# 448-row contractions as 64-row matmuls, four accumulators at a time, in a fused attention and MLP kernel

## The chip, the cores and the metric

One core of one Trainium2 chip. Times are device microseconds of one execution. Runs come in a fast and a slower state. The engines are TensorE (PE; its weight loads are PEld), VectorE (DVE), ScalarE (ACT), GpSimd (POOL) and SyncE (SP).

A ratio below is the mean time of one kernel's fast runs over that of the other's fast runs of the same rounds. It is not quite the ratio of the medians, which are quoted beside it.

## The reference

Cut to what matters; 2048 tokens, width 448, MLP width 1792, 16 heads of 28.

```python
xn = layernorm(x)
q, k, v = split(xn @ wqkv)                    # 448-row contractions
pq, pk = phi(q), phi(k)                       # phi(t) = t+1 if t>0 else exp(t)
kv, z = pk^T v, sum(pk)                       # over all tokens, per head
s = (pq kv / pq z) @ wo
h = relu(xn @ w1 + b1) ** 2                   # 448-row contraction
g = silu(h @ w2 + b2)
out = x + s * g
```

## The kernel before

The kernel records operations, and a small list scheduler gives each accumulator (`Buf`) one of eight banks of PSUM, the memory that matmuls write. A bank is free again when the last reader of its accumulator is done; such a reading out is called an evacuation below. One operation of PE is a run of matmuls. Its waits, those for banks included, come before its first matmul, and its semaphore is raised once, after its last:

```python
new = [b for b in op.writes if isinstance(b, Buf) and b.bank is None]
...
    banks = [b for _, b in times[: len(new)]]      # all of them free before the start
    r = max(r, times[len(new) - 1][0])
...
for op in self.order[e]:
    for s, v in waits[op]:
        h.wait_ge(s, v)
    op.emit(h, e).then_inc(op.sem, 16 if op.nbytes else 1)
```

448 rows are three times 128 and once 64. Two accumulators are made together, so that their 64-row leftovers lie in opposite halves of the array and run at the same time. Pairs alternate between halves last and halves first, so that the halves of two pairs meet:

```python
def pe_two(a, b, n, mm, reads, first):
    ...
    def f(e, _):                                   # halves last
        for w in (0, 1):
            for c in range(3):
                mm(e, w, full, c, c == 0, False)   # 128 rows
        mm(e, 0, lo, 3, False, True)               # 64 rows, lower half, bank a
        return mm(e, 1, hi, 3, False, True)        # 64 rows, upper half, bank b
    add("pe", f, reads, [a, b], 7 * MM(n) + 0.05)
```

The tokens go through in four groups of 512: k and v per 128 tokens, q, then fourteen blocks of h. In the middle of each group the kv product of that group (`kvt(g)`) is added to an accumulator that stays in its bank from group 0 until its mask is applied in group 3. So seven banks are left for the rest. ACT empties h (relu) and v (copy). For q and k the bank is read twice, by an exp on ACT and, after a minimum on DVE, by a multiply-maximum on DVE. After the groups come the denominators (`den`), the w2 products (`gg`), the division (`spread`) and the output products (`ss`).

Of the kernel before, what the change touches and what calls it, by code (L numbers as in the profile page):

```python
# [6 lines left out]
ALU = mybir.AluOpType  # L7
AF = mybir.ActivationFunctionType

P = 128  # L10
S, D, F = 2048, 448, 1792
NT, NG, NF = S // 128, S // 512, F // 128
NH, DH = 16, 28
HC = 4
PD = 112
KA = PD + HC

SPLIT64 = True
# [21 lines left out]
class Program:  # L40
# [8 lines left out]
    def add(self, eng, emit, reads=(), writes=(), dur=0.2, alts=(), nbytes=0):  # L49
        op = Op(eng, emit, reads, writes, dur, alts, nbytes)  # L50
        for t in op.reads:
            w = self.writer.get(t)
            if w is not None:
                op.raw.add(w)
            self.readers.setdefault(t, []).append(op)
        for t in op.writes:
            w = self.writer.get(t)
            if w is not None and w is not op:
                op.deps.add(w)
            for r in self.readers.get(t, ()):  # L60
                if r is not op:
                    op.deps.add(r)
            self.writer[t] = op
            self.readers[t] = [r for r in self.readers.get(t, ()) if r is op]
        op.raw.discard(op)
        op.deps |= op.raw
        for d in op.deps:
            d.succ.append(op)
        self.ops.append(op)
        return op  # L70
# [194 lines left out]
def bass_recurrent_scan__linear_attn_block__dense_activation_squared_relu__prompt_kernel(  # L265
    nc, A_x, A_wqkv, A_wo, B_x, B_w1, B_b1, B_w2, B_b2, out
):
    with ExitStack() as es:
# [3 lines left out]
        add = pr.add  # L272
# [9 lines left out]
        xT = sb("xT", [P, 4, S], bf)  # L282
        w_qkv = sb("w_qkv", [P, 4, 3 * D], bf)
        w_1 = sb("w_1", [P, 4, F], bf)
# [3 lines left out]
        b1f = sb("b1f", [P, NF], f32)  # L288
# [6 lines left out]
        pqT = sb("pqT", [P, 4, S], bf)  # L295
        pk = sb("pk", [P, NT, D], bf)
        va = sb("va", [P, NT, 4, KA], bf)
        r2 = sb("r2", [P, NF, S], bf)
# [5 lines left out]
        obuf = sb("obuf", [P, 8, D], bf)  # L304
        pbank = [es.enter_context(nc.psum_tensor(f"pb{i}", [P, 512], f32)) for i in range(PSUM_BANKS)]

        ps = lambda b: pbank[b.bank]


# [184 lines left out]

        MM = lambda n: n / 2400 + 0.003

        def pe_two(a, b, n, mm, reads, first):

            if not SPLIT64:
                for w, buf in ((0, a), (1, b)):  # L500

                    def f(e, _, w=w):
                        for c in range(4):
                            last = mm(e, w, slice(0, PD), c, c == 0, c == 3)
                        return last

                    add("pe", f, reads, [buf], 4 * MM(n))
                return
            lo, hi, full = slice(0, 64), slice(64, 128), slice(0, 128)
            if first:  # L510

                def f(e, _):
                    mm(e, 0, lo, 3, True, False)
                    mm(e, 1, hi, 3, True, False)
                    for c in range(3):
                        last = mm(e, 0, full, c, False, c == 2)
                    return last

                def f2(e, _):
                    for c in range(3):  # L520
                        last = mm(e, 1, full, c, False, c == 2)
                    return last

                add("pe", f, reads, [a, b], 4 * MM(n) + 0.05)
                add("pe", f2, reads, [b], 3 * MM(n))
            else:

                def f(e, _):
                    for w in (0, 1):
                        for c in range(3):  # L530
                            mm(e, w, full, c, c == 0, False)
                    mm(e, 0, lo, 3, False, True)
                    return mm(e, 1, hi, 3, False, True)

                add("pe", f, reads, [a, b], 7 * MM(n) + 0.05)

        flip = [False]

        def nextflip():
            flip[0] = not flip[0]  # L540
            return not flip[0]

        def phi(buf, slot, tile, rows, n):

# [18 lines left out]
            )  # L563

        def kv(si):
            kb, vb = Buf("K"), Buf("V")

            def mm(e, w, rows, c, start, stop):
                col = D * (1 + w)
                return e.matmul(  # L570
                    ps((kb, vb)[w])[:, 0:D], xT[rows, c, si * P : (si + 1) * P], w_qkv[rows, c, col : col + D],
                    start=start, stop=stop,
                )

            pe_two(kb, vb, D, mm, [("xT", si)] + wnames("wqkv"), nextflip())
            phi(kb, pk[:, si, :], ("pk", si), P, D)
            add(
                "act",
                lambda e, _: e.activation(
                    out=va[:, si, :, 0:PD], in_=ps(vb)[:, 0:D].rearrange("p (c j) -> p c j", c=4), func=AF.Copy  # L580
                ),
                [vb], [("va", si)], 0.547,
            )

        def qq(g, m):
            bufs = (Buf("Q"), Buf("Q"))

            def mm(e, w, rows, c, start, stop):
                col = (m + w) * PD
                return e.matmul(  # L590
                    ps(bufs[w])[0:PD, 0:512], w_qkv[rows, c, col : col + PD], xT[rows, c, g * 512 : (g + 1) * 512],
                    start=start, stop=stop,
                )

            pe_two(*bufs, 512, mm, [("xT", 4 * g + i) for i in range(4)] + wnames("wqkv"), nextflip())
            for w in (0, 1):
                phi(bufs[w], pqT[0:PD, m + w, g * 512 : (g + 1) * 512], ("pq", g, m + w), PD, 512)

        def hh(g, f0):
            bufs = (Buf("H"), Buf("H"))  # L600

            def mm(e, w, rows, c, start, stop):
                col = (f0 + w) * P
                return e.matmul(  # L604
                    ps(bufs[w])[:, 0:512], w_1[rows, c, col : col + P], xT[rows, c, g * 512 : (g + 1) * 512],
                    start=start, stop=stop,
                )

            pe_two(*bufs, 512, mm, [("xT", 4 * g + i) for i in range(4)] + wnames("w1"), nextflip())
            for w in (0, 1):  # L610
                fi = f0 + w
                slot = r2[:, fi, g * 512 : (g + 1) * 512]
                add(
                    "act",
                    lambda e, _, fi=fi, slot=slot, buf=bufs[w]: e.activation(  # L615
                        out=slot, in_=ps(buf)[:, 0:512], func=AF.Relu, bias=b1f[:, fi : fi + 1]
                    ),
                    [bufs[w], "b1f"], [("r2", g, fi)], 0.688,
                )

                def sq(e, eng, slot=slot):
                    if eng == "dve":
                        return e.tensor_tensor(out=slot, in0=slot, in1=slot, op=ALU.mult)  # L623
                    return e.activation(out=slot, in_=slot, func=AF.Square)

                add("dve", sq, [("r2", g, fi)], [("r2", g, fi)], 0.422)

        kvb = Buf("KV")

# [164 lines left out]
        bb = Buf("B1")  # L794
        add("pe", lambda e, _: e.transpose(ps(bb)[:, 0 : NF // 2].bitcast(bf), b1r[:, :], ident[0:NF, 0:NF]), ["b1r", "ident"], [bb], 0.1)
        add("dve", lambda e, _: e.tensor_copy(b1f[:, :], ps(bb)[:, 0 : NF // 2].bitcast(bf)), [bb], ["b1f"], 0.2)
        for g in range(NG):
            if g == 0:
                kv(0)
                for si in range(1, 4):  # L800
                    pe_transpose([si])
                    kv(si)
                qq(0, 0)
                qq(0, 2)
            else:
                qq(g, 0)
                for si in range(4 * g, 4 * g + 4):
                    kv(si)
                qq(g, 2)
            if g + 1 < NG:  # L810
                for si in range(4 * g + 4, 4 * g + 8):
                    ln_stats(si)
                ln_rstd(4 * g + 4, 4 * g + 8)
                for si in range(4 * g + 4, 4 * g + 8):
                    ln_norm(si)
                ln_twin(4 * g + 4, 4 * g + 8)
            for k in range(NF // 2):
                hh(g, 2 * k)
                if g + 1 < NG and k in (4, 5):
                    pe_transpose([4 * g + 4 + 2 * (k - 4), 4 * g + 5 + 2 * (k - 4)])  # L820
                if k == 2:
                    kvt(g)
                    if g == NG - 1:
                        kv_mask()
                if g == NG - 1 and k == 4:
                    for c in range(4):
                        fold_wo(c)
                if g == NG - 1 and k == 6:
                    den()
        gg(0)  # L830
        spread(0)
        gg(1)
# [42 lines left out]
```

## Time and profile before

| | before |
|---|---|
| median | 172.3 us (4 runs, 170.85 to 172.66) |
| profiled span | 169.7 us |
| PE busy | 155.1 us, 91% |
| groups 1 and 2 | 22.3 and 22.5 us |
| denominators' first matmul to the end | 62.6 us |

The page's first two parts: busy time by engine, and each engine's busy share in tenths over 40 slices of the span (PEclk is the granted clock).

```profile
PE 155.1 (91%) x913; PEld 74.8 (44%) x913; DVE 102.5 (60%) x246; ACT 76.7 (45%) x130; POOL 24.7 (15%) x42
PE   6327889999999999999999999979999999999990
PEclk9956999999999999999999999999999999999999
```

The chain of work that ended last, one middle group (start us, duration us, what). Here L590 is q, L570 k and v, L604 h, L635 the kv product and L475 the transposes for the next group.

```profile
40.27 1.65 PE pb L590 x8
41.91 5.72 PE pb L570 x32
47.64 1.65 PE pb L590 x8
49.28 4.85 PE pb L604 x24
54.14 0.85 PE pb L635 x16
54.99 3.23 PE pb L604 x16
58.22 0.45 PE pb L475 x8
```

Waits of PE (who waited for whom: us in total, times, longest; a fifth line, 1.6 us at the very start, is left out):

```profile
PE pb L475 <- DVE xn L455: 5.4, 1, 5.4
PE pb L570 <- ACT xT L488: 1.7, 2, 1.1
PE pb L704 <- ACT rden L693: 1.1, 1, 1.1
PE pb L570 <- DVE xT L487: 1.0, 2, 0.5
```

The chain goes from PE to PE with no gap, and PE's only waits are at the start and once before the division. So TensorE bounds the groups. What a change there can win has to be read from the starts of single matmuls, since the ends of matmuls in a trace are modelled. From the records of the trace between 40 and 105 us:

```
before: from -> to                          start to start (median, ns)
128 rows, 512 columns -> same               216
128 rows, 448 columns -> same               189
64 rows, lower half -> 64 rows, upper half  4
128 rows -> 64 rows (512 columns)           311
64 rows -> 128 rows (512 columns)           308
```

Two halves share one slot, but each change between 64-row and 128-row matmuls (a mode change, below) costs about 95 ns.

### The profile page before, as it was taken

How to read it: one execution, taken by the hardware profiler on the slowest of the kernel's cores; microseconds unless marked ns; L12 is line 12 of the kernel's file. 1: busy time of each engine (PE TensorE's matmuls, PEld its weight loads, DVE VectorE, ACT ScalarE, POOL GpSimd, SP SyncE). 2: the span in 40 equal slices, each digit the busy share in tenths (PEclk: the TensorE clock that was granted, in tenths of full speed). 3: DMA queues.
4: the chain of work that ended last, by engine and by line, in shares of the span. 5: the costliest groups of instructions: out<-in, count | busy, mean ns of one | idle time of the engine just before them, and what ended most of it. 6: DMA issues, size and time to landing. Idle time of an engine off the chain costs nothing.

```text
span 169.7 us, 2373 instructions
## 1 busy us (share of the span) xinstructions
PE 155.1 (91%) x913; PEld 74.8 (44%) x913; DVE 102.5 (60%) x246; ACT 76.7 (45%) x130; POOL 24.7 (15%) x42
## 2 busy tenths in 40 slices
PE   6327889999999999999999999979999999999990
PEld 6312444544345444435544354434455555555550
DVE  0186789938898466674667657469944432344263
ACT  3013357666577566756677566981211211112110
POOL 8620200210000000000000000000002244222442
PEclk9956999999999999999999999999999999999999
DMA  5999930000000000000000000000000010010003
GB/s 158 336 416 311 379 96 0 0 0 4 0 2 0 0 4 0 0 0 0 4 0 0 2 0 4 0 0 0 0 4 27 27 54 27 32 53 27 27 28 134
DMA packets 6598, 9.15 MB, mean 54 GB/s; under 512 B 508, under 2 KB 5052, under 8 KB 6588
## 3 DMA queue, kind: packets, MB, share of 16 engines
q1 hardware_dynamic: 6028, 7.63, 13.5%
q10 hardware_dynamic: 560, 1.38, 2.3%
q8 instruction: 7, 0.11, 0.3%
q14 instruction: 3, 0.02, 0.0%
HBM read 7.17 MB, written 1.84 MB: 53 GB/s over the span
## 4 chain that ended last, share of the span: by engine, by line
PE 85%; ACT 5%; DMA 4%; DVE 3%; issue 0%; SPq 0%; DVEq 0%
PE pb L604 26%; PE pb L725 24%; PE pb L570 14%; PE pb L590 8%; PE pb L749 7%; DMA x_tok<-in_A_x_dram 4%; PE pb L475 2%; PE pb L635 2%; ACT r L615 1%; DVE st L412 1%; PE pb L704 1%; ACT L693 1%; ACT L689 1%; ACT xT L488 1%; ACT pk L547 1%; PE pb L658 1%
## 5 line engine op out<-in xcount | busy, mean ns | idle before, releaser
L604 PE MATMUL pb<-xT,w 128*128 128x512 bf16 (+1 forms) x224 | 47.8, 381 | 0.0
L725 PE MATMUL pb<-w,r 128*128 128x448 bf16 x224 | 44.9, 353 | 0.0
L615 ACT ACTIVATE r<-pb,b1f 128x512 bf16<-128x512 f32 x56 | 35.2, 687 | 18.7 <-PE pb L604 18.7
L763 POOL TENSOR_TENSOR obuf<-obuf,x_tok 128x448 bf16<-128x448 bf16 x14 | 14.3, 1033 | 113.8 <-DVE obuf L758 113.8
L725 PEld LDWEIGHTS pb<-w,r 128*128 128x128 bf16 x224 | 21.5, 98 | 20.9 <-issue 1.3
L623 DVE TENSOR_TENSOR r<-r 128x512 bf16<-128x512 bf16 x56 | 22.9, 420 | 12.6 <-ACT r L615 12.6
L604 PEld LDWEIGHTS pb<-xT,w 128*128 128x128 bf16 (+1 forms) x224 | 17.2, 97 | 26.4 <-issue 10.9
L570 PE MATMUL pb<-w_qkv,xT 128*128 128x448 bf16 (+1 forms) x128 | 25.4, 367 | 2.7 <-ACT xT L488 1.7
L738 ACT ACTIVATE gbuf<-gbuf 128x448 bf16<-128x448 bf16 x16 | 9.2, 577 | 40.8 <-DVE gbuf L734 40.8
L734 DVE TENSOR_TENSOR gbuf<-pb,b2b 128x448 bf16<-128x448 f32 x16 | 10.0, 624 | 25.3 <-PE pb L725 25.0
L570 PEld LDWEIGHTS pb<-w_qkv,xT 128*128 128x128 bf16 (+1 forms) x128 | 10.0, 99 | 16.8 <-issue 6.9
L590 PE MATMUL pb<-xT,w_qkv 128*112 128x512 bf16 (+1 forms) x64 | 14.3, 387 | 0.0
L547 ACT ACTIVATE pk<-pb 128x448 bf16<-128x448 f32 x16 | 8.7, 546 | 12.1 <-PE pb L570 12.1
L412 DVE BATCH_NORM_STATS2 st<-x_tok 128x6 f32<-128x448 bf16 x16 | 9.4, 614 | 7.8 <-DMA x_tok<-in_A_x_dram 7.8
L749 PE MATMUL pb<-msb,pqT 112*128 112x448 bf16 x64 | 13.9, 352 | 0.0
L758 DVE TENSOR_TENSOR obuf<-pb,gbuf 128x448 bf16<-128x448 f32 x16 | 10.0, 624 | 2.1
L559 DVE SCALAR_TENSOR_TENSOR pqT<-pb,pqT 112x512 bf16<-112x512 f32 x16 | 10.7, 685 | 0.2
L547 ACT ACTIVATE pqT<-pb 112x512 bf16<-112x512 f32 x16 | 8.8, 596 | 4.4 <-PE pb L590 4.3
L475 PE MATMUL pb<-ident,xn 128*128 128x128 bf16 x64 | 5.6, 230 | 5.4 <-DVE xn L455 5.4
L712 DVE TENSOR_TENSOR pqT<-pqT,pb 112x512 bf16<-112x512 bf16 x16 | 9.9, 679 | 0.9 <-PE pb L704 0.9
L559 DVE SCALAR_TENSOR_TENSOR pk<-pb,pk 128x448 bf16<-128x448 f32 x16 | 9.9, 619 | 0.2
L590 PEld LDWEIGHTS pb<-xT,w_qkv 128*112 128x112 bf16 (+1 forms) x64 | 6.9, 129 | 6.5 <-issue 3.1
(56 smaller groups left out, 88.9 us busy)
## 6 DMA issues: line engine op xcount, KB each, us to landing
out_dram<-obuf SPq DMA_DIRECT2D x16, 112.0 KB, 1.7
w<-in_B_w_dram SPq DMA_DIRECT2D x1, 1568.0 KB, 16.7
x_tok<-in_A_x_dram SPq DMA_DIRECT2D x3, 448.0 KB, 12.0
w<-in_B_w_dram SPq DMA_DIRECT2D x1, 1344.0 KB, 11.5
w_qkv<-in_A_wqkv_dram ACTq DMA_DIRECT2D x1, 1008.0 KB, 6.2
w<-in_B_w_dram SPq DMA_DIRECT2D x2, 224.0 KB, 11.6
w_o<-in_A_wo_dram SPq DMA_DIRECT2D x1, 392.0 KB, 17.3
x_tok<-in_A_x_dram SPq DMA_DIRECT2D x1, 336.0 KB, 7.6
```

What stands on the lines that cost most here:

```text
L412: add("dve", lambda e, _: e.bn_stats(st6[:, si, :], x_tok[:, si, :]), [("x", si)], [("st", si)], 0.553)
L547: "act", lambda e, _: e.activation(out=slot, in_=ps(buf)[0:rows, 0:n], func=AF.Exp), [buf, "actw"],
L559: lambda e, _: e.scalar_tensor_tensor(out=slot, in0=ps(buf)[0:rows, 0:n], scalar=1.0 + 1e-6, in1=slot, op0=ALU.add, op1=ALU.max),
L570: return e.matmul(ps((kb, vb)[w])[:, 0:D], xT[rows, c, si * P : (si + 1) * P], w_qkv[rows, c, col : col + D], start=start, stop=stop,)
L590: return e.matmul(ps(bufs[w])[0:PD, 0:512], w_qkv[rows, c, col : col + PD], xT[rows, c, g * 512 : (g + 1) * 512], start=start, stop=stop,)
L604: return e.matmul(ps(bufs[w])[:, 0:512], w_1[rows, c, col : col + P], xT[rows, c, g * 512 : (g + 1) * 512], start=start, stop=stop,)
L615: lambda e, _, fi=fi, slot=slot, buf=bufs[w]: e.activation(out=slot, in_=ps(buf)[:, 0:512], func=AF.Relu, bias=b1f[:, fi : fi + 1]),
L623: return e.tensor_tensor(out=slot, in0=slot, in1=slot, op=ALU.mult)
L725: last = e.matmul(ps(b)[:, 0:D], r2[:, fi, si * P : (si + 1) * P], w_2[:, fi, :], start=(fi == 0), stop=(fi == NF - 1),)
L734: "dve", lambda e, _: e.tensor_tensor(out=gs, in0=ps(b)[:, 0:D], in1=b2b[:, :], op=ALU.add),
L749: last = e.matmul(ps(b)[:, 0:D], pqT[0:PD, c, si * P : (si + 1) * P], msb[0:PD, c, 0:D], start=(c == 0), stop=(c == 3),)
L763: return e.tensor_tensor(out=ob, in0=ob, in1=x_tok[:, si, :], op=ALU.add)
```

## The change

It removes those mode changes. Every contraction is cut into seven pieces of 64 rows, and four accumulators make a quad of 14 steps, each of one lower-half and one upper-half matmul. The halves always write different banks: first the lower half works on accumulators 0 and 1 while the upper half works on 2 and 3, then they swap. A semaphore guards the swap. kv quads are K, V, K, V; q and h quads are of four, or two and two.

```diff
+        def pe_four(units, n):
+            half = (slice(0, 64), slice(64, 128))
+            steps = ([], [])
+            for h in (0, 1):
+                first, second = (units[0:2], units[2:4])[:: 1 - 2 * h]
+                for u in first:
+                    steps[h].extend((u, c, c == 0, False) for c in range(4))
+                for u in second:
+                    steps[h].extend((u, c, False, c == 2) for c in range(3))
+            def f(e, _):
+                ...
+                for i in range(14):
+                    for h in (0, 1):
+                        u, c, start, stop = steps[h][i]
+                        if i in (8, 11):
+                            e.wait_ge(s_half, base + (2 if i == 8 else 4))
+                        last = u[2](e, half[h], c, start, stop)
+                        if i in (3, 7):
+                            last.then_inc(s_half, 1)
+                return last
+            ...
+            add("pe", f, reads, [u[0] for u in units], 14 * MM(n) + 0.1)
+            for u in units:
+                u[3]()                               # the evacuations
...
-                kv(0)
-                for si in range(1, 4):
-                    pe_transpose([si])
-                    kv(si)
+                pe_transpose([1])
+                pe_four(kv(0) + kv(1), D)
+                pe_transpose([2])
+                pe_transpose([3])
+                pe_four(kv(2) + kv(3), D)
...  (the other groups likewise; transposes and kv products between quads)
```

More of the change, by code (lines that the diff above doesn't have):

```diff
@@ L305, in bass_recurrent_scan__linear_attn_block__dense_activation_squared_relu__prompt_kernel @@
         pbank = [es.enter_context(nc.psum_tensor(f"pb{i}", [P, 512], f32)) for i in range(PSUM_BANKS)]
+        s_half = es.enter_context(nc.semaphore("s_half"))
+        quads = [0]
         ps = lambda b: pbank[b.bank]
@@ L495, in bass_recurrent_scan__linear_attn_block__dense_activation_squared_relu__prompt_kernel @@
         MM = lambda n: n / 2400 + 0.003
-        def pe_two(a, b, n, mm, reads, first):
-            if not SPLIT64:
-                for w, buf in ((0, a), (1, b)):
-                    def f(e, _, w=w):
-                        for c in range(4):
-                            last = mm(e, w, slice(0, PD), c, c == 0, c == 3)
-                        return last
-                    add("pe", f, reads, [buf], 4 * MM(n))
-                return
-            lo, hi, full = slice(0, 64), slice(64, 128), slice(0, 128)
-            if first:
-                def f(e, _):
-                    mm(e, 0, lo, 3, True, False)
-                    mm(e, 1, hi, 3, True, False)
-                    for c in range(3):
-                        last = mm(e, 0, full, c, False, c == 2)
-                    return last
-                def f2(e, _):
-                    for c in range(3):
-                        last = mm(e, 1, full, c, False, c == 2)
-                    return last
-                add("pe", f, reads, [a, b], 4 * MM(n) + 0.05)
-                add("pe", f2, reads, [b], 3 * MM(n))
-            else:
-                def f(e, _):
-                    for w in (0, 1):
-                        for c in range(3):
-                            mm(e, w, full, c, c == 0, False)
-                    mm(e, 0, lo, 3, False, True)
-                    return mm(e, 1, hi, 3, False, True)
-                add("pe", f, reads, [a, b], 7 * MM(n) + 0.05)
@@ L537, in bass_recurrent_scan__linear_attn_block__dense_activation_squared_relu__prompt_kernel @@
-        flip = [False]
-        def nextflip():
-            flip[0] = not flip[0]
-            return not flip[0]
+        def pe_four(units, n):
[8 more added lines that the diff above has]
+            def f(e, _):
+                last = None
+                base = quads[0]
+                quads[0] += 4
+                for i in range(14):
[7 more added lines that the diff above has]
+                return last
+            reads = []
+            for u in units:
+                reads += [r for r in u[1] if r not in reads]
+            add("pe", f, reads, [u[0] for u in units], 14 * MM(n) + 0.1)
+            for u in units:
+                u[3]()
@@ L566, in kv, with mm_of @@
             kb, vb = Buf("K"), Buf("V")
-            def mm(e, w, rows, c, start, stop):
-                col = D * (1 + w)
-                return e.matmul(
-                    ps((kb, vb)[w])[:, 0:D], xT[rows, c, si * P : (si + 1) * P], w_qkv[rows, c, col : col + D],
+            reads = [("xT", si)] + wnames("wqkv")
+            def mm_of(buf, col):
+                return lambda e, rows, c, start, stop: e.matmul(
+                    ps(buf)[:, 0:D], xT[rows, c, si * P : (si + 1) * P], w_qkv[rows, c, col : col + D],
@@ L572, in mm, with v_out @@
                     start=start, stop=stop,
                 )
-            pe_two(kb, vb, D, mm, [("xT", si)] + wnames("wqkv"), nextflip())
-            phi(kb, pk[:, si, :], ("pk", si), P, D)
-            add(
-                "act",
-                lambda e, _: e.activation(
-                    out=va[:, si, :, 0:PD], in_=ps(vb)[:, 0:D].rearrange("p (c j) -> p c j", c=4), func=AF.Copy
-                ),
-                [vb], [("va", si)], 0.547,
-            )
+            def v_out():
+                add(
+                    "act",
+                    lambda e, _: e.activation(
+                        out=va[:, si, :, 0:PD], in_=ps(vb)[:, 0:D].rearrange("p (c j) -> p c j", c=4), func=AF.Copy
+                    ),
+                    [vb], [("va", si)], 0.547,
+                )
@@ L585, in qq, with mm @@
+            return [
+                (kb, reads, mm_of(kb, D), lambda: phi(kb, pk[:, si, :], ("pk", si), P, D)),
+                (vb, reads, mm_of(vb, 2 * D), v_out),
+            ]
         def qq(g, m):
-            bufs = (Buf("Q"), Buf("Q"))
-            def mm(e, w, rows, c, start, stop):
-                col = (m + w) * PD
+            b = Buf("Q")
+            def mm(e, rows, c, start, stop):
                 return e.matmul(
-                    ps(bufs[w])[0:PD, 0:512], w_qkv[rows, c, col : col + PD], xT[rows, c, g * 512 : (g + 1) * 512],
+                    ps(b)[0:PD, 0:512], w_qkv[rows, c, m * PD : (m + 1) * PD], xT[rows, c, g * 512 : (g + 1) * 512],
@@ L592, in mm @@
                     start=start, stop=stop,
                 )
-            pe_two(*bufs, 512, mm, [("xT", 4 * g + i) for i in range(4)] + wnames("wqkv"), nextflip())
-            for w in (0, 1):
-                phi(bufs[w], pqT[0:PD, m + w, g * 512 : (g + 1) * 512], ("pq", g, m + w), PD, 512)
-        def hh(g, f0):
-            bufs = (Buf("H"), Buf("H"))
-            def mm(e, w, rows, c, start, stop):
-                col = (f0 + w) * P
+            reads = [("xT", 4 * g + i) for i in range(4)] + wnames("wqkv")
@@ L604, in mm, with hh @@
+            return b, reads, mm, lambda: phi(b, pqT[0:PD, m, g * 512 : (g + 1) * 512], ("pq", g, m), PD, 512)
+        def hh(g, fi):
+            b = Buf("H")
+            def mm(e, rows, c, start, stop):
                 return e.matmul(
-                    ps(bufs[w])[:, 0:512], w_1[rows, c, col : col + P], xT[rows, c, g * 512 : (g + 1) * 512],
+                    ps(b)[:, 0:512], w_1[rows, c, fi * P : (fi + 1) * P], xT[rows, c, g * 512 : (g + 1) * 512],
                     start=start, stop=stop,
@@ L607, in mm, with out @@
                 )
-            pe_two(*bufs, 512, mm, [("xT", 4 * g + i) for i in range(4)] + wnames("w1"), nextflip())
-            for w in (0, 1):
-                fi = f0 + w
+            def out():
                 slot = r2[:, fi, g * 512 : (g + 1) * 512]
@@ L614, in hh @@
                     "act",
-                    lambda e, _, fi=fi, slot=slot, buf=bufs[w]: e.activation(
-                        out=slot, in_=ps(buf)[:, 0:512], func=AF.Relu, bias=b1f[:, fi : fi + 1]
+                    lambda e, _: e.activation(
+                        out=slot, in_=ps(b)[:, 0:512], func=AF.Relu, bias=b1f[:, fi : fi + 1]
                     ),
-                    [bufs[w], "b1f"], [("r2", g, fi)], 0.688,
+                    [b, "b1f"], [("r2", g, fi)], 0.688,
                 )
-                def sq(e, eng, slot=slot):
-                    if eng == "dve":
-                        return e.tensor_tensor(out=slot, in0=slot, in1=slot, op=ALU.mult)
-                    return e.activation(out=slot, in_=slot, func=AF.Square)
-                add("dve", sq, [("r2", g, fi)], [("r2", g, fi)], 0.422)
+                add(
+                    "dve", lambda e, _: e.tensor_tensor(out=slot, in0=slot, in1=slot, op=ALU.mult), [("r2", g, fi)],
+                    [("r2", g, fi)], 0.422,
+                )
+            return b, [("xT", 4 * g + i) for i in range(4)] + wnames("w1"), mm, out
         kvb = Buf("KV")
@@ L796, in bass_recurrent_scan__linear_attn_block__dense_activation_squared_relu__prompt_kernel @@
         add("dve", lambda e, _: e.tensor_copy(b1f[:, :], ps(bb)[:, 0 : NF // 2].bitcast(bf)), [bb], ["b1f"], 0.2)
+        h_of = lambda g, lo, hi: [hh(g, fi) for fi in range(lo, hi)]
+        q_of = lambda g, lo, hi: [qq(g, m) for m in range(lo, hi)]
         for g in range(NG):
             if g == 0:
-                kv(0)
-                for si in range(1, 4):
-                    pe_transpose([si])
-                    kv(si)
-                qq(0, 0)
-                qq(0, 2)
-            else:
-                qq(g, 0)
-                for si in range(4 * g, 4 * g + 4):
-                    kv(si)
-                qq(g, 2)
+                pe_transpose([1])
[3 more added lines that the diff above has]
+                pe_four(kv(2) + kv(3), D)
+                pe_four(q_of(0, 0, 4), 512)
+                rest = [(0, 4), (4, 8), (8, 12)]
+            elif g % 2 == 1:
+                pe_four(h_of(g - 1, 12, 14) + q_of(g, 0, 2), 512)
+                pe_four(kv(4 * g) + kv(4 * g + 1), D)
+                pe_four(kv(4 * g + 2) + kv(4 * g + 3), D)
+                pe_four(q_of(g, 2, 4) + h_of(g, 0, 2), 512)
+                rest = [(2, 6), (6, 10), (10, 14)]
+            else:
+                pe_four(kv(4 * g) + kv(4 * g + 1), D)
+                pe_four(kv(4 * g + 2) + kv(4 * g + 3), D)
+                pe_four(q_of(g, 0, 4), 512)
+                rest = [(0, 4), (4, 8), (8, 12)]
             if g + 1 < NG:
@@ L816, in bass_recurrent_scan__linear_attn_block__dense_activation_squared_relu__prompt_kernel @@
                 ln_twin(4 * g + 4, 4 * g + 8)
-            for k in range(NF // 2):
-                hh(g, 2 * k)
-                if g + 1 < NG and k in (4, 5):
-                    pe_transpose([4 * g + 4 + 2 * (k - 4), 4 * g + 5 + 2 * (k - 4)])
-                if k == 2:
+            for k, (lo, hi) in enumerate(rest):
+                pe_four(h_of(g, lo, hi), 512)
+                if k == 0:
                     kvt(g)
@@ L824, in bass_recurrent_scan__linear_attn_block__dense_activation_squared_relu__prompt_kernel @@
                         kv_mask()
-                if g == NG - 1 and k == 4:
-                    for c in range(4):
-                        fold_wo(c)
-                if g == NG - 1 and k == 6:
-                    den()
+                if k == 1:
+                    if g + 1 < NG:
+                        pe_transpose([4 * g + 4, 4 * g + 5])
+                        pe_transpose([4 * g + 6, 4 * g + 7])
+                    else:
+                        for c in range(4):
+                            fold_wo(c)
+            if g == NG - 1:
+                den()
         gg(0)
```

## The prediction

> **What bounds it now.** TensorE. In the page's first part PE is busy 91% of a 169.7 us span, and the chain that ended last is 85% PE. The changed contractions lie at 12 to 105 us; a middle group of 512 tokens takes 22.3 us (chain: 40.27 to 62.56). From the starts of single matmuls in the timeline: a 128-row matmul follows the one before after 216 ns (512 columns) or 189 ns (448). Two 64-row matmuls on opposite halves start 3 to 4 ns apart, so they share one slot; but going into 64-row mode takes 311 ns instead of 216, and going out 308. A pair of accumulators therefore costs about 1.62 us (512) or 1.43 us (448: 5.72 us for four in the chain) where seven slots would be 1.51 or 1.32. The Trainium skill, "TensorEngine Tiling (Array Packing)", Key Properties, says that changing the tiling mode drains TensorE; this trace agrees, with about 95 ns per switch.
>
> **What the change removes.** Nearly all of these switches. Two adjacent 64-row pairs follow after 224 (512) or 197 ns (448), [...]so I estimate a slot of 218/191 ns and a quad of 14 slots at 3.05/2.68 us, against 3.24/2.86 for two pairs now. 18 quads of 512 columns and 8 of 448 save about 4.9 us. The added semaphore waits look back three or four slots and should cost nothing; more LDWEIGHTS stay hidden.
>
> **What it adds.** Each quad is one operation of the scheduler: it waits for four free PSUM banks before its first matmul, and its evacuations start after its last. Between the first kv product and its mask (nearly all of groups 0 to 3) that accumulator holds a bank, so seven remain. A quad has four, three are free, so the next must wait for the first bank of its predecessor to be evacuated. Pairs never had this: three fit into seven. The same skill page, Restrictions, warns that row tiling raises PSUM pressure.
>
> From the trace: the evacuation starts 0.41 us after the last matmul's start; a relu takes 0.69; so after an h quad the PE restarts 1.14 us later instead of 0.22: stall 0.92 us. After a kv quad, two exps go first (0.44 apart) and then the first copy (0.54): stall 1.7. After a quad with q: exp 0.60, min 0.29, multiply-max 0.69: stall 1.9. The kv product (0.85 us) fills one stall per group, transposes part of another. Sums, of estimates: group 1 8.9 us, group 2 7.0, group 3 7.8, group 0 about 2. The start loses 1 to 2 us more: the first quad needs two token tiles, so it starts near 17 us, on a halved clock (part 2: PEclk 5 to 6 tenths there now), instead of doing the first tile in the wait.
>
> All this is on the critical path; the second half (w2 and output products, 64 us) stays. Net: 27 + 1.5 - 4.9 = about +23 us.
>
> **Predicted: 195 us, 8 in 10 within 186 to 202.** Faster by over 2%: 5%; within 2%: 4%; slower: 91%.
>
> **Checks in the profile.** Single matmuls: 64-row slots of 216 to 220 ns with no 310 ns steps inside a quad. Waits: PE waiting for ACT and DVE evacuations, roughly 20 us or more in total, about 0.9 us after h quads and 1.7 to 1.9 after kv and q quads. PE busy share near 78 to 82%, with dips in the 40 slices between 40 and 130 us. Groups of 26 to 31 us. ACT and DVE busy sums unchanged.
>
> **What would make it wrong.** Slots of 228 ns (worse by 4 us), or DVE backlog lengthening stalls; or, the other way, banks coming free earlier than I think, so that stalls vanish and about 168 us remain.

## The result, and the profile after

| | before | after |
|---|---|---|
| median | 172.3 us | 195.37 us (4 runs, 194.61 to 195.8) |
| ratio | | 1.135, 95% interval 1.127 to 1.143 |
| PE busy | 155.1 us | 155.6 us |
| span before the denominators | 107.2 us | 126.9 us |
| span from them on | 62.6 us | 67.1 us |

The results of both kernels are correct. The first two parts of the page of the changed kernel:

```profile
PE 155.6 (80%) x1225; PEld 79.7 (41%) x1225; DVE 103.1 (53%) x248; ACT 73.5 (38%) x128; POOL 25.0 (13%) x42
PE   6238999766669985679866669894999999999992
PEclk9957999999999999999999999996699999999999
```

PE's busy time is the same, yet its share fell from 91% to 80%, and the slices between 35 and 130 us have holes that were not there. DVE and ACT do nearly the same work (102.5 and 103.1, 76.7 and 73.5 us). Waits of PE in the changed kernel (L561 is k and v, L584 q, L596 h, L569 the v copy, L549 the multiply-maximum, L605 the relu, L693 the division; the waits before 25 us and one of 0.6 us are left out):

```profile
PE pb L596 <- DVE pqT L549: 5.2, 3, 1.8
PE pb L561 <- ACT va L569: 4.5, 3, 1.5
PE pb L584 <- ACT va L569: 4.5, 3, 1.5
PE pb L596 <- ACT r L605: 3.2, 6, 0.8
PE pb L693 <- ACT rden L682: 2.7, 1, 2.7
PE pb L561 <- ACT r L605: 2.5, 2, 1.8
PE pb L561 <- DVE pqT L549: 1.7, 1, 1.7
```

All but that of L693 are waits for evacuations that free a bank, of which the kernel before had none. Whether too few banks or too slow engines are the cause is tested below. The chain of the changed kernel shows one of them whole: between two kv quads stand two exps and a copy of ACT.

```profile
101.12 2.84 PE pb L561 x28
103.99 0.98 ACT pk L537 x2
104.97 0.45 ACT va L569
105.41 0.05 issue
105.46 2.84 PE pb L561 x28
```

Single matmuls show the other side. From the records of the changed kernel's trace, last matmul of a quad to the first of the next, and steps inside a quad:

```
after: step                                   start to start (ns)
inside an h quad, step to step                216  (median; none above 260)
inside a kv quad, step to step                190
across a wait on the swap semaphore           216  (213 from the upper-half matmul before)
h quad -> any quad                            1155 to 1156
kv quad -> any quad                           1859 to 1862
quad with q -> any quad                       2119 to 2133
transposes -> h quad                          646 to 673
h quad -> kv product -> h quad                no idle time beyond the mode changes in
                                              groups 1 to 3; 592 at its end in group 0
```

To compare kernels I add up, from 25 us to the denominators, every such step in excess of the normal one (only steps over 300 ns between 64-row matmuls, or over 420 ns otherwise). I call this sum PE's stalls. It is 0 in the kernel before and 25.5 us in the changed one.

### The profile page after: what moved, and what is told of

Same layout as the page of the kernel before. It is cut to its first block, busy times and chain, and to the rows that moved or that the text cites. A ratio compares the mean times of both kernels' runs of the same rounds, so it can differ in the third digit from the quotient of the medians.

```text
span 193.9 us, 2992 instructions
## 1 busy us (share of the span) xinstructions
PE 155.6 (80%) x1225; PEld 79.7 (41%) x1225; DVE 103.1 (53%) x248; ACT 73.5 (38%) x128; POOL 25.0 (13%) x42
## 4 chain that ended last, share of the span: by engine, by line
PE 73%; ACT 13%; DVE 6%; DMA 4%; issue 1%; POOL 0%; SPq 0%; DVEq 0%
PE pb L596 23%; PE pb L714 22%; PE pb L561 12%; PE pb L584 6%; PE pb L738 6%; ACT r L605 5%; DMA x_tok<-in_A_x_dram 4%; ACT pk L537 3%; ACT pqT L537 2%; PE pb L624 2%; DVE pqT L549 1%; ACT va L569 1%; PE pb L693 1%; DVE st L414 1%; ACT L682 1%
## 5 line engine op out<-in xcount | busy, mean ns | idle before, releaser
L596 PE MATMUL pb<-xT,w 64*128 64x512 bf16 x392 | 51.2, 377 | 9.1 <-DVE pqT L549 5.2
L714 PE MATMUL pb<-w,r 128*128 128x448 bf16 x224 | 47.5, 367 | 0.0
L605 ACT ACTIVATE r<-pb,b1f 128x512 bf16<-128x512 f32 x56 | 34.2, 689 | 25.5 <-PE pb L596 25.5
L596 PEld LDWEIGHTS pb<-xT,w 64*128 64x128 bf16 x392 | 21.1, 94 | 30.6 <-DVE pqT L549 6.7
L561 PE MATMUL pb<-w_qkv,xT 64*128 64x448 bf16 x224 | 23.7, 362 | 10.1 <-ACT va L569 4.5
L714 PEld LDWEIGHTS pb<-w,r 128*128 128x128 bf16 x224 | 22.1, 101 | 22.8 <-issue 4.2
L584 PE MATMUL pb<-xT,w_qkv 64*112 64x512 bf16 x112 | 19.2, 378 | 4.5 <-ACT va L569 4.5
L561 PEld LDWEIGHTS pb<-w_qkv,xT 64*128 64x128 bf16 x224 | 10.6, 97 | 23.0 <-ACT va L569 5.9
L537 ACT ACTIVATE pk<-pb 128x448 bf16<-128x448 f32 x16 | 7.8, 541 | 20.7 <-PE pb L561 20.7
L584 PEld LDWEIGHTS pb<-xT,w_qkv 64*112 64x112 bf16 x112 | 10.4, 127 | 10.1 <-ACT va L569 5.9
L542 DVE TENSOR_SCALAR pqT<-pqT 112x512 bf16<-112x512 bf16 x16 | 4.4, 288 | 12.1 <-ACT pqT L537 12.1
L542 DVE TENSOR_SCALAR pk<-pk 128x448 bf16<-128x448 bf16 x16 | 4.3, 271 | 12.2 <-ACT pk L537 12.0
L549 DVE SCALAR_TENSOR_TENSOR pqT<-pb,pqT 112x512 bf16<-112x512 f32 x16 | 10.7, 684 | 0.1
```

Source lines behind the costliest of these rows:

```text
L537: "act", lambda e, _: e.activation(out=slot, in_=ps(buf)[0:rows, 0:n], func=AF.Exp), [buf, "actw"],
L549: lambda e, _: e.scalar_tensor_tensor(out=slot, in0=ps(buf)[0:rows, 0:n], scalar=1.0 + 1e-6, in1=slot, op0=ALU.add, op1=ALU.max),
L561: return lambda e, rows, c, start, stop: e.matmul(ps(buf)[:, 0:D], xT[rows, c, si * P : (si + 1) * P], w_qkv[rows, c, col : col + D], star ...
L584: return e.matmul(ps(b)[0:PD, 0:512], w_qkv[rows, c, m * PD : (m + 1) * PD], xT[rows, c, g * 512 : (g + 1) * 512], start=start, stop=stop,)
L596: return e.matmul(ps(b)[:, 0:512], w_1[rows, c, fi * P : (fi + 1) * P], xT[rows, c, g * 512 : (g + 1) * 512], start=start, stop=stop,)
L605: lambda e, _: e.activation(out=slot, in_=ps(b)[:, 0:512], func=AF.Relu, bias=b1f[:, fi : fi + 1]),
```

## Experiments

The theory (A): a quad asks for four of the seven free banks before its first matmul and returns all four only after its last. Three banks are free, so each quad waits for the first evacuation of the one before. Rivals: (B) ACT and DVE can not empty four accumulators per quad fast enough, whatever the granularity; (C) the 64-row mode, its weight loads or its semaphores are slow. The steps inside quads already speak against C.

### e1: the quad in four operations

The matmuls and their order stay. Two banks are asked for at step 0, the other two at step 4; accumulators 0 and 2 are released after step 10, the others after step 13. (The swap then waits on the operations' own semaphore for one half, because a part's last matmul already raises that one. The code cut shows only the operations.)

```diff
-            add("pe", f, reads, [u[0] for u in units], 14 * MM(n) + 0.1)
+            parts.append(add("pe", part(0, 4), reads, [units[j][0] for j in (0, 2)], 4 * MM(n) + 0.1))
+            parts.append(add("pe", part(4, 8), reads, [units[j][0] for j in (1, 3)], 4 * MM(n)))
+            parts.append(add("pe", part(8, 11), reads, [units[j][0] for j in (0, 2)], 3 * MM(n)))
+            parts.append(add("pe", part(11, 14), reads, [units[j][0] for j in (1, 3)], 3 * MM(n)))
```

> Each quad is cut into four operations of the scheduler: two banks are asked for at the first matmul, the other two at the ninth (0.86 us later), and two accumulators are released 0.65 us before the end; the matmuls and their order stay. Theory A (a quad takes four of seven banks at its first matmul and gives them back only after its last): the bank that comes free 1.14 us (h), 1.4 (k, v) or 1.5 us (q) after a quad is now wanted only at about 1.0 to 1.1 us, so nearly all of the 24 us of stalls go; time 173 to 178 us. Theory B (ACT and DVE can not empty four accumulators per quad fast enough, whatever the granularity): within 2% of the changed kernel, 192 to 197. Theory C (64-row matmuls or the semaphores inside a quad are slow): also no gain, 192 to 197.

Measured: 170.21 us (169.57 without its slow run), ratio to the kernel before 0.989 (0.981 to 0.996), stalls 2.2 us. Its waits of PE after the start are small, except the one before the division:

```profile
PE pb L707 <- ACT rden L696: 2.1, 1, 2.1
PE pb L575 <- ACT va L583: 0.6, 3, 0.2
PE pb L610 <- DVE pqT L563: 0.2, 1, 0.2
```

The same engines do the same work, and 23 us of stalls are gone. B and C fall, since both forbade a gain. It came out 3 us below the expected range, because the expectation left out the tail, which is also shorter here (63.5 us against 67.1; see e6).

### e2 and e3: one half of e1 each

```diff
 e2, ask late, release at the end:
+            parts.append(add("pe", part(0, 4), reads, [units[j][0] for j in (0, 2)], 4 * MM(n) + 0.1))
+            parts.append(add("pe", part(4, 14), reads, [units[j][0] for j in (0, 1, 2, 3)], 10 * MM(n)))
 e3, ask at the start, release early:
+            parts.append(add("pe", part(0, 11), reads, [units[j][0] for j in (0, 1, 2, 3)], 11 * MM(n) + 0.1))
+            parts.append(add("pe", part(11, 14), reads, [units[j][0] for j in (1, 3)], 3 * MM(n)))
```

> Only the first half of e1: banks three and four are asked for at the ninth matmul, the release stays at the end. A: 0.86 us (0.76 in kv quads) of each stall is hidden, h stalls vanish, kv stalls fall from 1.7 to about 0.9 and q stalls from 1.9 to about 1.1: about 14 us less, 179 to 184 us. B and C: 192 to 197.

> Only the other half: all four banks at the first matmul, but two accumulators are released three slots (0.65 us, 0.57 in kv quads) before the end. A: about 0.5 to 0.65 us less per boundary, 8 to 9 us in all: 185 to 189 us. B and C: 192 to 197.

Measured: e2 180.23 us (ratio 1.049), stalls 10.8 us, as expected. e3 181.67 us (ratio 1.055), stalls 13.4 us; 3 us better than expected. After an h quad e3 stalls 0.30 us and after a kv quad 1.10, close to what the 0.65 us allow. But its four quads with both q and h release an h block early, which one relu empties, so that the stall after them is 0.78 us and not the 1.26 us that the quad of q alone has. Its tail is also 3.6 us shorter, which I had not counted. Both halves are worth having, and neither is enough alone.

### e4: eight banks instead of seven

Whole quads, but all four kv products in group 3, so that no accumulator is held before.

```diff
-                    kvt(g)
                     if g == NG - 1:
+                        for gk in range(NG):
+                            kvt(gk)
                         kv_mask()
```

> The changed kernel with whole quads, but all four parts of the kv product are done in group 3, so that its accumulator holds no bank in groups 0 to 2: eight banks instead of seven, two full quads. The work of every engine is the same. A: most stalls before group 3's kv product vanish (about 20 us), some remain after q quads (DVE still busy with the quad before last) and at the transposes, which need a bank too; the kv product no longer fills stalls: 173 to 180 us. B: no gain from a bank, 190 to 197. C: 192 to 197.

Measured: 174.07 us, ratio 1.010 (1.003 to 1.016), stalls 5.0 us. With the quads untouched, one bank takes away 20 of the 25.5 us. This is the strongest evidence for A: nothing about an engine's load has changed. Its waits of PE after the start, without those for the division:

```profile
PE pb L596 <- ACT r L605: 2.1, 3, 0.9
PE pb L596 <- DVE xT L489: 0.7, 2, 0.3
PE pb L596 <- DVE msb L654: 0.6, 1, 0.6
PE pb L561 <- DVE pqT L549: 0.2, 1, 0.2
```

Of the 5.0 us that are left, 1.5 stand at the transposes, which need a bank too, and 2.1 where the kv product no longer fills the wait after the first h quad (groups 0 and 2). The rest are two short waits between kv quads and one for the products of `wo` (L654).

### e5: the same quads of 128-row matmuls

```diff
+                a, b, c4, d = units
+                for u in (a, b):
+                    for c in range(3):
+                        u[2](e, full, c, c == 0, False)
+                a[2](e, half[0], 3, False, True)
+                b[2](e, half[1], 3, False, True)
+                c4[2](e, half[0], 3, True, False)
+                d[2](e, half[1], 3, True, False)
+                for u in (c4, d):
+                    for c in range(3):
+                        last = u[2](e, full, c, False, c == 2)
```

> The changed kernel's quads (four banks at the first matmul, four accumulators released after the last), but made of the matmuls of the kernel before: twelve of 128 rows and two pairs of halves in the middle. No 64-row accumulation across halves and no semaphore inside a quad. Theory A (the loss is the quad's four banks, not the 64-row mode): the same stalls of 0.9 to 1.9 us, and each quad 0.19 us longer for its two mode switches, less about 1.3 us for switches that transposes and kv products no longer need: 197 to 201 us. Theory C (the 64-row mode or its semaphores cost the time): near the kernel before, 172 to 178.

Measured: 198.7 us, ratio 1.157, stalls 25.8 us. The stalls are there without any accumulation across halves and without a swap semaphore, so C falls again. The run also tells what the 64-row mode is worth among equal stalls. The whole times differ by 198.7 - 195.4 = 3.3 us, but the tails differ as well: 65.8 us in the trace of e5 and 67.1 in that of the changed kernel, whose clock is halved there for 6.8 us and not for 3.4. Up to the denominators e5 takes 131.7 us and the changed kernel 126.9, which is 4.8 us, 0.3 of it stalls. So the mode is worth about 4.5 us.

### e6 and e7: the tail

After the last relus ACT makes the reciprocal denominators (table load, Ln, table load, Exp) while PE does one w2 product and then waits. A second w2 product goes first:

```diff
         gg(0)
+        gg(1)
         spread(0)
-        gg(1)
+        gg(2)
         spread(1)
-        gg(2)
  ...
```

> The changed kernel, with a second w2 product done before the first spread, so that PE has work while ACT makes the reciprocal denominators. If the 3 us that the tail lost against the prediction are this wait (3.08 us after the first w2 product, 1.46 in the kernel before) and the halved clock after it: 2.9 us less, up to 4.5 where the clock had dropped: 190 to 193 us. If the tail is longer for another reason: 194 to 196.

> The same exchange in the kernel before, whose wait there is 1.46 us instead of 0.2: 1.0 to 1.3 us less, 170.5 to 171.5 us, ratio 0.992 to 0.995. If the wait is off the critical path: no change.

The chain in the tail of the kernel before, then in that of the changed kernel (L725 and L714 are the w2 products):

```profile
105.66 2.42 ACT r L615 x4
108.10 1.28 ACT L689
110.10 1.28 ACT L693
112.50 2.76 PE pb L725 x14
```

```profile
126.97 2.42 ACT r L605 x4
129.42 1.28 ACT L678
131.42 1.28 ACT L682
134.07 5.34 PE pb L714 x14
```

The relus of the last four h blocks start before the last pair has ended in the kernel before, and only after the whole quad in the changed one. From the start of the last matmul of the first w2 product to that of the division it takes 1.46 us in the one and 3.08 in the other (as idle time the profile counts 1.1 and 2.7). The second w2 product then takes 5.34 instead of 2.76 us in the changed kernel: the clock records of its trace have 0.5 from 132.7 to 139.5 us.

e6 measured 190.89 us (ratio 1.111 to the kernel before; the changed kernel had 1.135), 4.5 us below the changed kernel; its tail takes 61.5 us instead of 67.1. With the same exchange the tail of the kernel before (e7) takes 61.4, so the changed kernel's excess is this wait and the clock. e7 measured 171.52 us, ratio 0.998 (0.993 to 1.003): the expected gain is not resolved. Its profiled run shows the tail 1.2 us shorter (61.4 against 62.6 us), but that run's first group was slower, with matmuls of 448 columns 348 to 374 ns apart for stretches until 21.0 us, so its span is no shorter (169.8 us).

### e8 and e9: a version below both

e8 is e1, with V before K in kv quads (so that the accumulators released early are those that one copy empties) and the tail of e6. e9 has 130 instead of 40 warming matmuls as well.

```diff
 e8:  return [
+         (vb, reads, mm_of(vb, 2 * D), v_out),
          (kb, reads, mm_of(kb, D), lambda: phi(...)),
-         (vb, reads, mm_of(vb, 2 * D), v_out),
      ]
 e9: -        warm(40)
     +        warm(130)
```

> Candidate: e1 (quads in four parts), with v before k in its quads, so that the accumulators released early are those that one ACT copy empties, and the tail exchange of e6. e1 still waits 0.28 to 0.35 us in the middle of each quad that follows a kv quad (about 1.9 us in all) and 2.43 us for the denominators. Theory A: 165 to 168 us, below both kernels. If those small waits are DVE backlog instead of bank order: 167 to 170.

> e8 with 130 instead of 40 warming matmuls before the first transpose. In e8 the first kv quad runs at a halved clock for part of its 14 slots because TensorE idles for six microseconds before it. If the clock at the start depends on that idle time: the first quad falls to about 2.5 us and the time by 1.3 to 2 us against e8, 163.5 to 165 us. If the halved clock is not due to the idle time, or if the start waits for the input in any case: no change, 165 to 166.5.

e8: 165.73 us (6 runs, 165.21 to 166.51), ratio 0.966 (0.961 to 0.971): faster than the kernel before by 3.4%, with stalls of 0.6 us. Its page:

```profile
PE 150.4 (92%) x1225; PEld 78.5 (48%) x1225; DVE 101.5 (62%) x246; ACT 74.4 (45%) x130; POOL 25.0 (15%) x42
PE   6217899999999999999999999999999999999990
```

e9: 165.84 us, ratio 0.963 (0.957 to 0.969), no difference from e8. In its trace the clock holds until 14.7 us instead of 7.8, but is 0.5 from 14.7 to 18.1 us all the same, amid waits of 1.5, 1.1 and 1.6 us for the first tiles, so that the first kv quad still has steps of 368 to 373 ns. The expectation took for granted that the idle time (6.2 us in the trace of e8) halves the clock. What the two traces show is less: more warming moved the drop of the clock, but did not spare the quad.

## Why the prediction was right

It said 195 us (186 to 202), and 195.37 was measured. The mechanism was the one that e1 to e5 show. Point by point:

- **Slots.** Estimated 218 and 191 ns, measured 216 and 190. No mode change inside a quad, and the swap waits cost nothing. Right.
- **Stall at each boundary.** Restart estimated 1.14 us after an h quad, measured 1.155; after kv 1.9 (0.19 and a stall of 1.7), measured 1.86; after q 2.1, measured 2.12 to 2.13. Group 1, with seven quads, took 31.35 us (38.45 to 69.80) and group 2, with six, 26.35 us (69.80 to 96.15): inside the 26 to 31 of the checks or just above. Right, because the durations were taken from the same evacuations in the trace before.
- **Sum of the stalls.** The text's four group sums, 2, 8.9, 7.0 and 7.8 us, add to 25.7, and it then carried 27 without saying why. Measured were 2.1, 8.7, 6.8 and 7.9, together 25.5. The parts were right, and 27 was 1.5 us too much.
- **What the 64-row mode saves.** Estimated 4.9 us, measured about 4.5 (e5). A second count agrees: from the first q matmul to the denominators the kernel before takes 83.9 us and the changed one 104.6, only 20.7 more with 25.5 us of stalls, so 4.7 us were saved. Some mode changes stay, on each side of a kv product and of the transposes (306 ns in place of 216 going out, 149 in place of 53 coming back): after 25 us there are 17, where the kernel before has 56. Right.
- **The start.** "Loses 1 to 2 us more" was wrong. The first kv quad started at 14.26 us, not 17, because the second tile's transposes no longer wait behind a kv product, and q began at 22.25 us instead of 23.29. The start gained about 1 us.
- **The tail.** "The second half stays" was wrong: 67.1 instead of 62.6 us, by the wait of 3.08 us for the denominators and the halved clock after it. It is the same cause as the stalls, four accumulators released at once, at the one place where I had not looked for it.

The misses cancel: 1.5 us too much in the sum and a start better by 2.5 us than said stand against a tail worse by 4.5. That the total came within 1 us is therefore luck; that it lies well inside the range is not, since the stalls, by far the largest term, were right one by one. Counted in spans, stalls of 25.5 less 4.5 for the mode (e5) less 1 for the start make 20.0 us, and the span before the denominators grew by 19.7.

Of the skill's pages, "TensorEngine Tiling (Array Packing)" was used twice. Its Key Properties say that changing the tiling mode drains TensorE: such a change costs here 92 to 96 ns. Its Restrictions and Gotchas (PSUM Pressure) say that row tiling raises PSUM pressure. A shortage of banks is indeed the main cost here, with 25.5 us of stalls, but it did not come from row tiling: e5 has 25.8 us of them with mostly 128-row matmuls, so it is the four banks at once that press.

## What to carry to other kernels

Before work is grouped into larger units, count the banks: a unit that takes more than half of what is free can not be double-buffered, and then every unit pays the latency of its predecessor's first evacuation unless other work lies between, here 0.9 to 1.9 us, even though no evacuating engine is near its limit (ACT was busy for 38% of the time, DVE for 53%). Ask for a bank when its first matmul needs it and release it when its last is done (e1), or free a bank held for long elsewhere (e4). Either brought the time back to about that of the kernel before (ratios 0.989 and 1.010); clearly faster were only e8 and e9 (0.966 and 0.963), which also put V before K and change the tail. And look at what a later release does at the end of a phase: a PE wait that grew from 1.5 to 3.1 us there also went with a halved clock.

## What the Trainium skill lacked or had wrong

- "TensorEngine Tiling (Array Packing)", Key Properties: the drain at a change of tiling mode has no number. Here a change between 128-row and 64-row matmuls of 512 columns made the step 306 to 319 instead of 216 ns.
- "TensorEngine Tiling (Array Packing)": no sustained rate for row tiling, with weights changed for every matmul. Here 28 matmuls on two halves, each with its own weight load, went at 216 ns (512 columns) and 190 ns (448) per pair, as a 128-row matmul does.
- "TensorEngine Tiling (Array Packing)", PSUM Pressure: it does not say that the number of banks asked for at once decides. With the same matmuls, stalls were 25.5 us with whole quads and seven banks, 5.0 with eight banks, 2.2 with quads in parts.
- "TensorE: Matmul & The Clock Gate", LDWEIGHTS: it gives a time that grows with the columns. Here loads of 112 columns took 127 to 130 ns and those of 128 columns 93 to 98 (medians). Its section on Fast Weight Load, which asks for 128 weights, may be the reason, which no run tested; the two are not put together there. No run here shows that it costs time in a steady stream.
- "TensorE: Matmul & The Clock Gate", Part 1, on the idle window of about 3.4 us: the clock records here do come in stretches of 3.4 us and its multiples. Before the division, 1.46 and 2.43 us from matmul to matmul (kernel before, e1) left the clock alone, and 3.08 us, less than a window, went with a halved clock for 3.4 us (e2, e4, e5) or 6.8 us (the changed kernel). The page's closing table, which sets the limit at about 3 us, fits this better. The length of one wait is not all: in e9 the clock fell amid waits of 1.5, 1.1 and 1.6 us close together.
- None has it in this form: the clock row of a profile can be blind at the start. The traces of e1, e3 and e7 hold no clock record before 17.35, 17.27 and 20.99 us, and their pages show full clock there, yet matmuls of 448 columns are up to 369 to 374 ns apart in that time. The steps of the matmuls tell, the row does not.
